# Part of a fused attention and feed-forward kernel in 512-token blocks, its second product further behind, and its first two slots interleaved

## The chip, the core and the metric

The kernel runs on one core of a Trainium2 chip. The time is device microseconds of the whole program, as the median of several runs. A profile shows one execution in detail; its span, from the first instruction to the last, is some 2 us shorter than the time, since starting and ending the program are not in it.

## What is computed

The reference is a sliding-window attention followed by a feed-forward layer with a smooth ReLU:

```python
B, H, S, D = 8, 8, 576, 64                 # q, k, v
scores = q @ k.T / sqrt(D), kept where |i - j| <= 32
attn = softmax(scores) @ v
x = attn.transpose(0, 2, 1, 3).reshape(4608, 512)
h = x @ w_in                               # 512 -> 2048
g = where(h >= 1, h, where(h <= -1, 0, (h + 1) ** 2 / 4))
out = g @ w_out                            # 2048 -> 512
```

The inputs and the output are float32; the kernel multiplies in bfloat16 and sums in float32.

## The kernel before

**The feed-forward part.** x is kept transposed, xT (128 partitions, 4 groups of the 512 features, and a ring of 2304 tokens, which is 4 batches). The work is divided into blocks of 256 tokens (t, 18 of them) and, in each, eight steps f of 256 of the 2048 hidden features. One block and one step are a *slot*, a = 8 t + f, 144 slots in all, written out in the loop at L482. In a slot:

- TensorE makes hp, 2 x 128 hidden features by 256 tokens, with 8 matmuls of 256 columns (L504). hp has two buffers in ps_h (one bank each); slot 6 takes one of ps_o's.
- ScalarE makes rr = relu(hp / 2 + 1/2) (L508), and VectorE makes mx = max(hp, rr) (L515) and gT = min(rr, 1) * mx (L516), which is the smooth ReLU. In the slots of two_on_act ScalarE squares rr (L512) and VectorE needs one operation (L513).
- TensorE multiplies earlier gT by w_out, 8 slots behind: in slot a a *quarter* a - 8, four of the 16 matmuls of 512 columns that one output tile of 128 tokens needs (L444). Early blocks go in half widths, pair (L460). When a tile is complete ScalarE copies it (L449), and SP's queue stores it. gT has three buffers of 256 tokens; op, the product's accumulator, has two.

The last eight rounds of the loop, slots 144 to 151, have the second product alone; the very last tile is made in two halves (L433), so that the first half's store is under way while the second is computed.

**Attention.** It is cut into steps that are hung onto slots in a table, at(slot, ...). A step is one `sums` (the product of weights and v, and the sum of weights, L293; then ln and exp(-x) on ScalarE, L299 and L300, for the reciprocal; then VectorE writes xT, L305, or L308 in a batch's last step) and one `scores` of the step after (L227; exp on ScalarE, L235; the mask on VectorE, L201). A batch has five: tokens 0 to 223 for two pairs of heads, 224 to 479 for two pairs, and 480 to 575 for all. The list sl gives the slots of the steps from number 6 on. TensorE's order within a slot is hp, sums, scores, quarter. VectorE's order is mx and gT of the slot, the mask, then, at the next flush(), xT, and only then the next slot's mx. ScalarE's order is rr, exp, ln, exp(-x), the output copy, the next rr. [...]

**Loads.** GpSimd issues all loads that turn float32 into bfloat16 (q, k, v, w_in, w_out), in one queue, at most eight in flight; those of the later batches are issued in the slots of the table `loads`, and SP transposes q and k by DMA (xps), 6 and 8 slots later. Both tables are tied to sl.

**The start.** Half of batch 0's first two head rows is loaded first, transposed on TensorE and used for slots 0 and 1 alone: casts of q, transposes of q and k, copies out of PSUM (L190), the scores with the mask added as a bias (add_mask, L206), sums, and xT for 256 tokens in two parts, y = 0 and y = 1. Matmuls on a tile of zeros (keep_warm, L336) fill TensorE's time between: 11, 3, 4, 2 and 7. v of batch 0 comes in four loads (L106), then w_in's columns by 256, the rest of batch 0's q and k, more of w_in (columns 512 to 767 for slot 2, 768 to 1023 for slot 3, 1024 to 1535 in two larger loads for slots 4 and 5, and so on), and w_out.

Of the kernel before, what the change touches and what calls it, by code (L numbers as in the profile page):

```python
# [7 lines left out]
FP = mybir.dt.float32  # L8
BF = mybir.dt.bfloat16
# [5 lines left out]
def kernel(  # L15
# [19 lines left out]
    nc = tc.nc  # L35
# [6 lines left out]
    TAIL = S - MAIN  # L42
    RING = 4 * S
    PAD = 32
    LONG = 2

    const = ctx.enter_context(tc.tile_pool(name="const", bufs=1))
# [2 lines left out]
    ptp = ctx.enter_context(tc.tile_pool(name="ptp", bufs=2))  # L50
    smp = ctx.enter_context(tc.tile_pool(name="smp", bufs=2))
    ewp = ctx.enter_context(tc.tile_pool(name="ewp", bufs=3))
    gtp = ctx.enter_context(tc.tile_pool(name="gtp", bufs=3))
    osp = ctx.enter_context(tc.tile_pool(name="osp", bufs=3))
    ps_h = ctx.enter_context(tc.tile_pool(name="ps_h", bufs=2, space=bass.MemoryType.PSUM))
    ps_s = ctx.enter_context(tc.tile_pool(name="ps_s", bufs=1, space=bass.MemoryType.PSUM))
# [11 lines left out]
    w_in = const.tile([128, 4, DFF], BF, name="w_in")  # L68
    w_out = const.tile([128, 16, DM], BF, name="w_out")
    xT = const.tile([128, NY, RING], BF, name="xT")  # L70
    qTs = [const.tile([128, PAD + NY * S], BF, name=f"qT{i}") for i in range(3)]

    ctx.enter_context(tc.manual_schedule())
# [24 lines left out]
            nc.gpsimd.dma_start(out=x[:, :, h], in_=src[b, NY * h:NY * h + NY].rearrange("y s d -> (y s) d")  # L98
                                .rearrange("(u p) d -> p u d", p=128))

    def load_v(b, n):
        if b not in vn:
            vn[b] = nat.tile([128, 2 * NC, 2, D], BF, name="vn", tag="vn", bufs=3)
        h, a = divmod(n, 2)
        y = NY * h + 2 * a
        nc.gpsimd.dma_start(out=vn[b][64 * a:64 * a + 64, :, h], in_=v[b, y:y + 2].rearrange("y s d -> (y s) d")  # L106
                            .rearrange("(c r) d -> r c d", r=64))

    def load_w_in(c0, c1, h):
        nc.gpsimd.dma_start(out=w_in[64 * h:64 * h + 64, :, c0:c1],  # L110
# [20 lines left out]
    P.affine_select(out=step, in_=step, compare_op=ALU.is_ge, fill=-1.0, base=-65, channel_multiplier=-1,  # L131
                    pattern=[[1, 257]])
    for n in range(4):
        load_v(0, n)
    V.memset(ones, 1.0)
    for t in qTs:
        V.memset(t[:, 0:PAD], 0.0)
# [4 lines left out]
    def put(todo):  # L142
        for fn, *x in todo:
            fn(*x)
# [1 line left out]
    w = [(load_w_in, c, c + 256, h) for c in range(0, 1024, 256) for h in range(2)]  # L146
    w += [(load_w_in, 1024, 1536, h) for h in range(2)]
    w += [(load_w_in, c, c + 256, h) for c in range(1536, DFF, 256) for h in range(2)]
    put(w[:4] + [(load_half, 1, t, h) for t in range(2) for h in range(2)] + w[4:12])
    put([(load_w_out, 0, 0, 4)] + w[12:])  # L150
    P.tensor_copy(band[HD[1], 0:128], band[HD[1], 64:192])
    for m, n, x in ((mask4, 8, 128), (mask8, 4, TAIL)):
# [55 lines left out]
                                 .to_broadcast([64, n, w]),  # L208
                                 start=True, stop=False, skip_group_check=True)

    def scores(b, ys, pars, cs, eng, pool=ps_s, w=128):

        if b not in pt:
            pt[b] = ptp.tile([128, 2, 2, 2, 512], BF, name="pt")
        ps = two_banks(pool)
        n = 0
        if eng is None:
            cols = (ys[1] - ys[0]) * (pars[1] - pars[0]) * (cs[1] - cs[0])
            add_mask([ps[:, h] for h in range(2)], cols, w)
        for y1 in range(*ys):  # L220
            for par in range(*pars):
                for c2 in range(*cs):
                    c = 2 * c2 + par
                    for a in range(2):
                        for h in range(2):
                            s0 = S * (y1 + 2 * a) + 64 * c
                            nc.tensor.matmul(ps[HD[a], h, w * n:w * n + w], kT[b][HD[h], s0:s0 + 64],  # L227
                                             qTs[b % 3][HD[h], PAD + s0 - 32:PAD + s0 - 32 + w],
                                             start=eng is not None, stop=True, skip_group_check=True)
                    n += 1  # L230
        p = pt[b][:, :, ys[0]:ys[1], pars[0]:pars[1], 128 * cs[0]:128 * cs[1] - 128 + w]
        m = 2 if n > cs[1] - cs[0] else 1
        p = p[:, :, ys[0] - ys[0]] if ys[1] - ys[0] == 1 else p[:, :, :, 0]
        like = "p h (y j) -> p h y j"
        A.activation(p, ps[:, :, :w * n].rearrange(like, y=m), AF.Exp, scale=D ** -0.5)  # L235
        mask(eng, p, mask4[:, :256 * n].rearrange("p (h j) -> p h j", h=2).rearrange(like, y=m))
# [79 lines left out]
    TB = 256  # L316
# [29 lines left out]
    with tc.tile_pool(name="ps_p", bufs=1, space=bass.MemoryType.PSUM) as ps_p:  # L346
        keep_warm(11, ps_h, "hp")

        V.memset(qkT(0, 0).rearrange("d (y s) -> d y s", y=NY)[:, :, S // 2:352], 0.0)
        for b in range(LONG):  # L350
            V.memset(qkT(b, 0).rearrange("d (y s) -> d y s", y=NY)[:, :, S - PAD:], 0.0)
        V.memset(qkT(0, 1).rearrange("d (y s) -> d y s", y=NY)[:, :, S // 2:320], 0.0)
        qn[0, 0] = cast(q32, "qb", 5)
        qq = [tpose(0, n, 0, (A.copy, V.tensor_copy)[n], tp1(ps_h)) for n in range(2)]
        for x in qq:
            x()
        kk = [tpose(0, n, 1, (A.copy, V.tensor_copy)[n], tp1((ps_n, ps_p)[n])) for n in range(2)]
        keep_warm(3, ps_h, "hp")
        for x in kk:
            x()  # L360
        scores(0, (0, 1), (0, 2), (0, 2), None)
        scores(0, (0, 2), (0, 1), (2, 3), None, ps_n, 32)
        scores(0, (1, 2), (0, 2), (0, 2), None, ps_p)
        keep_warm(4, ps_h, "hp")
        e0 = sums(0, 0, 0, TB)
        keep_warm(2, ps_h, "hp")
        e1 = sums(0, 1, 0, TB, ps_p)
        keep_warm(7, ps_h, "hp")
        e0()
        e1()  # L370
    ps_o = ctx.enter_context(tc.tile_pool(name="ps_o", bufs=2, space=bass.MemoryType.PSUM))
# [33 lines left out]
        at(a, seq[2 + n][0])  # L405
    for n, a in enumerate((18, 20, 26.5, 28)):
        at(a, seq[3 + n][1])
    sl = [30, 32, 35, 39, 42, 45, 49, 52, 56, 59, 62, 65, 69, 73, 77, 81, 84, 88, 92]
    sl += [96, 99, 103, 106, 110, 113, 116, 120, 124, 128]
    for n, a in enumerate(sl):  # L410
        at(a, seq[6 + n][0], seq[7 + n][1] if n < len(sl) - 1 else None)
    for t in range(2):
# [6 lines left out]
        for t in range(2):  # L419
            xps.setdefault(a + 6 + 2 * t, []).append((b, t))  # L420

    gT, op = {}, {}

    def quarter(x):

        tt, ff = divmod(x, 4)
        if tt == NT // 128 - 1:
            half, n = divmod(ff, 2)
            if n == 0:
                op[tt] = ps_o.tile([128, 256], FP, name="op", tag="op")  # L430
            cols = slice(256 * half, 256 * half + 256)
            for j in range(NF * n, NF * n + NF):
                nc.tensor.matmul(op[tt], gT[tt // 2][:, j, 128 * (tt % 2):128 * (tt % 2) + 128], w_out[:, j, cols],  # L433
                                 start=j == 0, stop=j == 2 * NF - 1)
            if n:
                osb = osp.tile([128, 256], FP, name="osb")
                A.copy(osb, op[tt])
                nc.sync.dma_start(out=out[128 * tt:128 * tt + 128, cols], in_=osb)
            return
        if tt not in op:  # L440
            op[tt] = ps_o.tile([128, DM], FP, name="op", tag="op"), []
        o, done = op[tt]
        for j in range(4 * ff, 4 * ff + 4):
            nc.tensor.matmul(o, gT[tt // 2][:, j, 128 * (tt % 2):128 * (tt % 2) + 128], w_out[:, j],  # L444
                             start=not done, stop=len(done) == 2 * NF - 1, skip_group_check=True)
            done.append(j)
        if len(done) == 2 * NF:
            osb = osp.tile([128, DM], FP, name="osb")
            A.copy(osb, o)  # L449
            nc.sync.dma_start(out=out[128 * tt:128 * tt + 128, :], in_=osb)  # L450

    def pair(x):
# [4 lines left out]
        o, done = op[half, p]  # L457
        for tt in range(2):
            for j in range(4 * g, 4 * g + 4):
                nc.tensor.matmul(o[:, tt], gT[p][:, j, 128 * tt:128 * tt + 128], w_out[:, j, 256 * half:256 * half + 256],  # L460
                                 start=not done, stop=len(done) == 4 * NF - 1, skip_group_check=True)
                done.append(j)
        if len(done) == 4 * NF:
# [15 lines left out]
        for end in todo:  # L479
            end()  # L480

    for a in range(NF * NB + NF):  # L482
        t, f = divmod(a, NF)
        eng = None if a < 14 else V
        post = [x for n, x in pairs if n == a] + [a - NF] * (a >= 2 * NF + 2)
        for b, x in loads.get(a, []):
            if x < 2:
                load_nat(b, x)
# [2 lines left out]
                    load_v(b, n)  # L491
        if a == 0 or a > 3:
            flush()
        if t < NB:
            if t not in gT:
                gT[t] = gtp.tile([128, 2 * NF, TB], BF, name="gT", tag="gT")
            r0 = TB * t % RING
            if a == 6:
                hp = ps_o.tile([128, 2, TB], FP, name="hp", tag="op")
            else:  # L500
                hp = ps_h.tile([128, 2, TB], FP, name="hp", tag="hp")
            for j in range(2):
                for n, kk in enumerate((0, 2, 1, 3)):
                    nc.tensor.matmul(hp[:, j], w_in[:, kk, 256 * f + 128 * j:256 * f + 128 * j + 128],  # L504
                                     xT[:, kk, r0:r0 + TB], start=n == 0, stop=n == 3)

            rr = ewp.tile([128, 2, TB], FP, name="rr")
            A.activation(rr, hp, AF.Relu, scale=0.5, bias=0.5)  # L508
            g = gT[t][:, 2 * f:2 * f + 2]
            mx = ewp.tile([128, 2, TB], FP, name="mx")  # L510
            if a in two_on_act:
                A.activation(mx, rr, AF.Square)  # L512
                V.scalar_tensor_tensor(g, hp, 1.0, mx, op0=ALU.max, op1=ALU.min)  # L513
            else:
                V.tensor_max(mx, hp, rr)  # L515
                V.scalar_tensor_tensor(g, rr, 1.0, mx, op0=ALU.min, op1=ALU.mult)  # L516
        flush()
        run(a)
        for x in post:
            (pair if x < 4 * 4 else quarter)(x)  # L520
        run(a + 0.5)
        for x in xps.get(a, []):
            xpose(*x)
# [30 lines left out]
```

The softmax here doesn't subtract the row's maximum and nothing guards it: scores larger than these inputs give would overflow.

## Time and profile before

| what | value |
|---|---|
| time, median of 3 runs | 308.69 us (308.67 to 309.4) |
| span of the profiled run | 306.7 us, granted TensorE clock 1.0 |
| busy: PE, DVE, ACT, POOL | 299.9, 242.1, 192.5, 77.4 us |
| hp, 256 columns (L504) | 1152 matmuls, 149.4 us busy |
| op, 512 columns (L444) | 496 matmuls, 126.9 us busy |
| gT's two operations on VectorE (L515, L516) | 137 each, 690 and 695 ns |
| rr on ScalarE (L508) | 144, 595 ns |
| idle time of TensorE that the waits view lists | 3.1 us |

A row's mean is the length of one instruction; matmuls are pipelined, so their lengths overlap, and the cost of one is better read from the distance of two starts. A group of the time line is named by its first start and the time to its last end, and what stands in brackets is the idle time of the engine before it and what ended that.

### The profile page before, as it was taken

What the parts mean: (1) busy time and instruction counts of PE and PEld (TensorE: products, weight loads), DVE (VectorE), ACT (ScalarE), POOL (GpSimd) and SP (SyncE); (2) the same over time, 40 slices, a digit from 0 to 9 for tenths busy, and PEclk for the clock granted to TensorE, in tenths of its full rate; (3) what the DMA queues carried; (4) which work ended last, traced back from release to release, by engine and by line L of the source; (5) the groups of instructions that cost most, each with busy time, mean ns of one, the idle gap of its engine ahead of it and who ended that gap; (6) DMA issues with size and microseconds to landing.
All of it is one profiled execution on the core that took longest, in us unless ns stands there. A gap on an engine that the chain in (4) does not pass through costs nothing.

```text
span 306.7 us, 8496 instructions
## 1 busy us (share of the span) xinstructions
PE 299.9 (98%) x3650; PEld 206.6 (67%) x3650; DVE 242.1 (79%) x376; ACT 192.5 (63%) x320; POOL 77.4 (25%) x92
## 2 busy tenths in 40 slices
PE   8989999999999999999999999999999999999995
PEld 3567878876666666666666666666666666666654
DVE  4278568888888888889888888889888888888760
ACT  3688886738856767666656666566676666554431
POOL 8799461028008106400450003700000000000000
PEclk9999999999999999999999999999999999999999
DMA  9999999999999999996899156990811010010111
GB/s 153 182 197 198 177 201 152 174 152 149 138 206 89 170 191 107 159 94 142 102 170 138 34 108 91 167 150 17 177 50 36 34 36 36 35 36 34 60 45 68
DMA packets 137173, 35.70 MB, mean 116 GB/s; under 512 B 122160, under 2 KB 132912, under 8 KB 137136
## 3 DMA queue, kind: packets, MB, share of 16 engines
q0 software_dynamic: 102976, 18.06, 83.2%
q1 hardware_dynamic: 34016, 16.81, 25.6%
q8 instruction: 28, 0.46, 0.6%
q10 hardware_dynamic: 144, 0.29, 0.3%
q14 instruction: 9, 0.07, 0.1%
HBM read 36.70 MB, written 9.44 MB: 150 GB/s over the span
## 4 chain that ended last, share of the span: by engine, by line
PE 89%; ACT 3%; DVE 2%; DMA 2%; issue 1%; POOL 1%; POOLq 0%; ACTq 0%
PE hp L504 39%; PE op L444 36%; PE bb L293 6%; PE op L460 4%; PE bb L227 2%; DMA vn<-in_v_dram 2%; PE op L433 1%; ACT pt L235 1%; POOL vn L106 1%; PE tp L187 1%; DVE xT L305 1%; ACT rc L300 1%; DVE mx L515 1%; ACT lr L299 1%; DVE gT L513 0%
## 5 line engine op out<-in xcount | busy, mean ns | idle before, releaser
L504 PE MATMUL hp<-xT,w_in 128*128 128x256 bf16 x1152 | 149.4, 273 | 1.7 <-DMA w_in<-in_moe_w_in_dram 0.8
L508 ACT ACTIVATE rr<-hp 128x512 f32<-128x512 f32 x144 | 85.7, 595 | 87.8 <-PE hp L504 87.7
L504 PEld LDWEIGHTS <-w_in 128*128 128x128 bf16 x1152 | 112.0, 98 | 41.1 <-issue 2.3
L444 PE MATMUL op<-w_out,gT 128*128 128x512 bf16 x496 | 126.9, 380 | 0.0
L515 DVE TENSOR_TENSOR mx<-hp,rr 128x512 f32<-128x512 f32 x137 | 94.5, 690 | 30.8 <-ACT rr L508 28.9
L516 DVE SCALAR_TENSOR_TENSOR gT<-rr,mx 128x512 bf16<-128x512 f32 x137 | 95.2, 695 | 4.7
L444 PEld LDWEIGHTS <-gT 128*128 128x128 bf16 x496 | 46.1, 98 | 34.8
L98 POOL DMA_DIRECT2D qn<-in_q_dram x12 | 14.6, 1221 | 111.4 <-DMA kT<-kn 107.5
L235 ACT ACTIVATE pt<-bb 128x1024 bf16<-128x1024 f32 (+1 forms) x33 | 32.7, 1002 | 5.0 <-PE bb L227 3.7
L305 DVE TENSOR_TENSOR xT<-bb,rc 128x512 bf16<-128x512 f32 (+1 forms) x32 | 21.0, 658 | 10.1 <-ACT rc L300 9.6
L106 POOL DMA_DIRECT2D vn<-in_v_dram x32 | 27.5, 891 | 4.9 <-DMA w_out<-in_moe_w_out_dram 4.2
L300 ACT ACTIVATE rc<-lr 128x512 f32<-128x512 f32 (+2 forms) x40 | 23.5, 587 | 1.3
L449 ACT COPY osb<-op 128x512 f32<-128x512 f32 x31 | 18.1, 583 | 8.7 <-PE op L444 8.3
L299 ACT ACTIVATE lr<-bb 128x512 f32<-128x512 f32 (+2 forms) x40 | 22.0, 551 | 0.4 <-PE bb L293 0.3
L201 DVE TENSOR_TENSOR pt<-pt,mask 128x1024 bf16<-128x1024 bf16 (+1 forms) x33 | 20.3, 614 | 0.5 <-ACT pt L235 0.5
L293 PE MATMUL bb<-pt,ones 64*64 64x256 bf16 (+3 forms) x352 | 19.6, 256 | 0.1
L293 PE MATMUL bb<-pt,vn 64*64 64x128 bf16 (+3 forms) x712 | 18.4, 204 | 0.1
L293 PEld LDWEIGHTS <-vn 64*64 64x64 bf16 x712 | 16.7, 107 | 0.3 <-DMA vn<-in_v_dram 0.3
L460 PE MATMUL op<-w_out,gT 128*128 128x256 bf16 x128 | 16.5, 273 | 0.0
L293 PEld LDWEIGHTS <-ones 64*64 64x64 bf16 x352 | 10.2, 105 | 8.9 <-issue 8.9
L98 POOL DMA_DIRECT2D kn<-in_k_dram x12 | 14.6, 1230 | 0.5 <-issue 0.5
L227 PE MATMUL bb<-qT,kT 64*64 64x128 bf16 (+1 forms) x520 | 13.1, 217 | 0.3 <-DVE kT L190 0.2
(59 smaller groups left out, 115.1 us busy)
## 6 DMA issues: line engine op xcount, KB each, us to landing
out_dram<-osb SPq DMA_DIRECT2D x35, 256.0 KB, 2.5
vn<-in_v_dram POOLq DMA_DIRECT2D x32, 144.0 KB, 10.2
qn<-in_q_dram POOLq DMA_DIRECT2D x12, 288.0 KB, 6.9
kn<-in_k_dram POOLq DMA_DIRECT2D x12, 288.0 KB, 8.9
w_in<-in_moe_w_in_dram POOLq DMA_DIRECT2D x12, 128.0 KB, 5.7
w_out<-in_moe_w_out_dram POOLq DMA_DIRECT2D x4, 256.0 KB, 6.6
w_out<-in_moe_w_out_dram POOLq DMA_DIRECT2D x2, 512.0 KB, 15.8
kh<-in_k_dram POOLq DMA_DIRECT2D x4, 144.0 KB, 5.1
```

Source lines behind the costliest of these rows:

```text
L98: nc.gpsimd.dma_start(out=x[:, :, h], in_=src[b, NY * h:NY * h + NY].rearrange("y s d -> (y s) d") .rearrange("(u p) d -> p u d", p=128))
L106: nc.gpsimd.dma_start(out=vn[b][64 * a:64 * a + 64, :, h], in_=v[b, y:y + 2].rearrange("y s d -> (y s) d") .rearrange("(c r) d -> r c d", ...
L235: A.activation(p, ps[:, :, :w * n].rearrange(like, y=m), AF.Exp, scale=D ** -0.5)
L293: nc.tensor.matmul(bb[HD[h], a, o + c0:o + c1], ones[HD[a]] if c is None else vn[b][HD[a], c, h], p(a, h), start=n == 0, stop=True, skip_g ...
L299: A.activation(lr[:, :, :D0], bb[:, :, D0:2 * D0], AF.Ln)
L300: A.activation(rc[:, :, :D0], lr[:, :, :D0], AF.Exp, scale=-1.0)
L444: nc.tensor.matmul(o, gT[tt // 2][:, j, 128 * (tt % 2):128 * (tt % 2) + 128], w_out[:, j], start=not done, stop=len(done) == 2 * NF - 1, s ...
L460: nc.tensor.matmul(o[:, tt], gT[p][:, j, 128 * tt:128 * tt + 128], w_out[:, j, 256 * half:256 * half + 256], start=not done, stop=len(done ...
L504: nc.tensor.matmul(hp[:, j], w_in[:, kk, 256 * f + 128 * j:256 * f + 128 * j + 128], xT[:, kk, r0:r0 + TB], start=n == 0, stop=n == 3)
L508: A.activation(rr, hp, AF.Relu, scale=0.5, bias=0.5)
L515: V.tensor_max(mx, hp, rr)
L516: V.scalar_tensor_tensor(g, rr, 1.0, mx, op0=ALU.min, op1=ALU.mult)
```

## The change

- WIDE = 72, 136: the slots from 72 to 135 work on two blocks of 256 tokens at a time. A slot is then 128 hidden features by 512 tokens: 4 matmuls of 512 columns. The number of slots, and the size of what ScalarE and VectorE do in each, stay.
- gT becomes one tile with room for four blocks of 256 tokens; home(t) says which of them block t has. In a wide slot VectorE writes two of them at once.
- The second product is divided into units, single matmuls. Up to slot 39 it goes as before. From slot 40 to 87 a slot has 4, 3 or 3 units in turn, then 4; so it is 8 slots behind at slot 40 and 16 from slot 88 on, and eight more rounds of the loop follow at the end.
- The steps of attention from number 14 on are 1 to 5 slots earlier (sl), and with them the loads and DMA transposes of batches 4 to 7.
- Slots 0 and 1 are made together: the parts with y = 0 of both, then the parts with y = 1 of both.
- The first bias (add_mask) is issued before k's copies are waited for; keep_warm is 11, 1, 3, 0 and 6.
- v of batch 0 is loaded in two parts, chunks 0 to 13 where it was, and chunks 14 to 17 after w_in's columns 512 to 767.

```diff
-    for n in range(4):
-        load_v(0, n)
+        load_v(0, n, 0, 14)
...
-    put(w[:4] + [(load_half, 1, t, h) for t in range(2) for h in range(2)] + w[4:12])
+    put(w[:4] + [(load_half, 1, t, h) for t in range(2) for h in range(2)]
+        + w[4:6] + [(load_v, 0, n, 14, 2 * NC) for n in range(4)] + w[6:12])
...
-        keep_warm(3, ps_h, "hp")
+        keep_warm(1, ps_h, "hp")
+        first = two_banks(ps_s)
+        add_mask([first[:, h] for h in range(2)], 4, 128)
         for x in kk:
             x()
-        scores(0, (0, 1), (0, 2), (0, 2), None)
+        scores(0, (0, 1), (0, 2), (0, 2), None, ready=first)
...
-        keep_warm(4, ps_h, "hp")
+        keep_warm(3, ps_h, "hp")
         e0 = sums(0, 0, 0, TB)
-        keep_warm(2, ps_h, "hp")
         e1 = sums(0, 1, 0, TB, ps_p)
-        keep_warm(7, ps_h, "hp")
+        keep_warm(6, ps_h, "hp")
...
-    sl = [30, 32, 35, 39, 42, 45, 49, 52, 56, 59, 62, 65, 69, 73, 77, 81, 84, 88, 92]
-    sl += [96, 99, 103, 106, 110, 113, 116, 120, 124, 128]
+    sl = [30, 32, 35, 39, 42, 45, 49, 52, 55, 58, 61, 64, 67, 70, 74, 77, 80, 84, 88]
+    sl += [91, 94, 97, 101, 105, 108, 111, 114, 118, 123]
...
+    def home(t):
+
+        return (3 - t % 4 if t % 4 in (0, 3) else t % 4) if WIDE[0] <= NF * t < WIDE[1] else t % 4
...
+        if j == 0:
+            op[tt] = ps_o.tile([128, DM], FP, name="op", tag="op")
+        nc.tensor.matmul(op[tt], gT[:, j, home(tt // 2), 128 * (tt % 2):128 * (tt % 2) + 128], w_out[:, j],
+                         start=j == 0, stop=j == 15)
...
+            if wide:
+                n, f = divmod(a - WIDE[0], 2 * NF)
+                t = WIDE[0] // NF + 2 * n
+                r0 = TB * t % RING
                 hp = ps_h.tile([128, 2, TB], FP, name="hp", tag="hp")
                 for n, kk in enumerate((0, 2, 1, 3)):
+                    nc.tensor.matmul(hp.rearrange("p n t -> p (n t)"), w_in[:, kk, 128 * f:128 * f + 128],
+                                     xT[:, kk, r0:r0 + 2 * TB], start=n == 0, stop=n == 3)
+                g = gT[:, f, home(t):home(t + 1) + 1:home(t + 1) - home(t)]
...
+                if a == 0:
+                    hps = [ps_h.tile([128, 2, TB], FP, name="hp", tag="hp") for _ in range(2)]
+                    for y in range(2):
+                        for f2 in range(2):
+                            project(hps[f2], f2, 0, [(j, y + 2 * m) for j in range(2) for m in range(2)], y == 0, y == 1)
...
+        if a >= 40:
+            n = (4, 3, 3)[a % 3] if a < 88 else 4
+            for x in range(done, done + n):
+                unit(x)
+            done += n
```

## The prediction

> **What bounds the kernel now.** I read four views in this order: the page (who is busy, and in which slices), TensorE's waits, the time line of the first 32 us, and the time lines of single slots later on.
>
> ```profile
> PE   8989999999999999999999999999999999999995
> PEclk9999999999999999999999999999999999999999
> DMA  9999999999999999996899156990811010010111
> ...
> L504 PE MATMUL hp<-xT,w_in 128*128 128x256 bf16 x1152 | 149.4, 273 | 1.7 <-DMA w_in<-in_moe_w_in_dram 0.8
> L444 PE MATMUL op<-w_out,gT 128*128 128x512 bf16 x496 | 126.9, 380 | 0.0
> ```
>
> TensorE has 9 in all slices but the first few and the last, at full clock; the DMA engines have 9 for the first 18 slices. So two things can set the end: TensorE's own work after the start, and, in the start, transfers. TensorE's waits over the whole span:
>
> ```profile
> PE z L336 <- DVE warm L126: 1.2, 1, 1.2
> PE hp L504 <- DMA w_in<-in_moe_w_in_dram: 0.8, 2, 0.6
> PE hp L504 <- DVE gT L513: 0.5, 1, 0.5
> PE hp L504 <- DVE xT L305: 0.4, 1, 0.4
> PE bb L227 <- DVE kT L190: 0.2, 1, 0.2
> ```
>
> Only 3.1 us, and TensorE's time line puts every one before 31 us. The last two that matter here are these:
>
> ```profile
> 22.39 1.03 PE L504 MATMUL hp<-xT,w_in 128*128 128x256 bf16 x8 [0.24 <-DMA w_in<-in_moe_w_in_dram]
> ...
> 30.30 1.03 PE L504 MATMUL hp<-xT,w_in 128*128 128x256 bf16 x8 [0.47 <-DVE gT L513]
> ```
>
> The first is slot 4, which waits for w_in's columns 1024 to 1535; the second is slot 9, which waits until VectorE has read slot 7's hp. From 30.30 to 303.3 us TensorE never waits to speak of; a stretch of the windows view shows who else is near:
>
> ```profile
> 60.00:80.00 20.00, 20.00 (x256) 14.21 (x254) 17.08 (x27) 13.19 (x22) 8.25 (x8) 1.00 1.70 156
> ```
>
> 20.00 of 20 us on PE, 17.08 on VectorE (third busy figure), 13.19 on ScalarE. Thus after 30.30 a microsecond of TensorE work is a microsecond of the end, unless an edit wakes a wait.
>
> [...] eight 256-column hp take 0.87 us to the next start, four 512-column op 0.86. [...] the longest gap here is 0.59 us and PEclk is 9 throughout, so leaving out six of the warm-up matmuls should not cost the clock.
>
> **The change part by part.**
>
> (1) 512-token blocks, slots 72 to 135. Each of 64 slots has 4 matmuls of 512 columns for 8 of 256: [...] 10 ns, times 64 = 0.64 us saved, all on the path. Weight loads halve, but PEld was busy 14.21 of 20 us and hidden. VectorE's and ScalarE's operations keep 128x512 elements; gT's new address pattern costs them nothing that I can see[...].
>
> (2) w_out up to 16 slots behind. From slot 40 to 87 a slot has 3.33 instead of 4 op matmuls; 32 matmuls move to after slot 151. TensorE's sum is the same. What was 1.737 us in a bare slot becomes 0.873 + 3.33 x 0.216 = 1.593 us, so VectorE must keep up. Three slots with one attention step cost TensorE 3 x 0.873 + 10 x 0.216 + 0.81 (the mean that an attention step adds to a slot, from five successive ones) = 5.59 us. VectorE, start to start when it has work: 1.33 us for mx and g (223.84 to 225.17), 0.60 for the mask, 0.54 for xT: 3 x 1.33 + 1.14 = 5.13. It fits, with 8% to spare. The end is as before: the last tile in two halves, copy, DMA. Nothing to add.
>
> (3) Attention earlier. The instant when an attention slot's scores are issued I call T (the next op's start). What follows is latency, not work:
>
> ```profile
> 94.70 1.04 PE L444 MATMUL op<-w_out,gT 128*128 128x512 bf16 x4
> ...
> 96.81 0.56 DVE L308 TENSOR_TENSOR xT<-bb,rc 128x384 bf16<-128x384 f32 x1
> ```
>
> This is slot 39, a batch's tail step (tokens 480 to 575). xT is done at 97.37 = T + 2.67: ScalarE's exp, ln and exp come first. In the new schedule the tail step of batch 4 is in slot 70, and slot 72 is the first wide block, tokens 2304 to 2815, that is up to token 511 of batch 4. It needs that xT. TensorE arrives there after 3 op, a hp block and 3 op: 6 x 0.216 + 0.873 = T + 2.17. The wait is 2.67 - 2.17 + 0.05 (the release, as from xT's end at 14.49 to hp at 14.54) = 0.55 us. The kernel before shows such a wait in small: slot 32 needs slot 30's xT,
>
> ```profile
> 78.81 0.62 DVE L305 TENSOR_TENSOR xT<-bb,rc 128x448 bf16<-128x448 f32 x1 [0.18 <-ACT rc L300]
> ...
> 79.20 1.10 PE L504 MATMUL hp<-xT,w_in 128*128 128x256 bf16 x8
> ```
>
> and its group lasts 1.10 instead of 1.04 us, though 8 op lie between instead of 6. Slot 120 has the same distance to slot 118, but there scores8's shorter exp, 8 op, and the rows that are needed third leave about 0.5 us; no wait. Where a step is 3 slots before, T + 3.9 meets xT at T + 3.0: none.
>
> The other buffer is hp: slot a+3 needs mx of slot a+1, which stands behind xT. In a full-width step without an output copy (slot 32, T = 81.03, mx to 84.65) mx ends at T + 3.62, against T + 10 x 0.216 + 2 x 0.873 = T + 3.91: none. With the output copy in the same slot it is later:
>
> ```profile
> 220.54 1.04 PE L444 MATMUL op<-w_out,gT 128*128 128x512 bf16 x4
> ...
> 222.74 0.57 ACT L449 COPY osb<-op 128x512 f32<-128x512 f32 x1
> ...
> 223.84 0.69 DVE L515 TENSOR_TENSOR mx<-hp,rr 128x512 f32<-128x512 f32 x1 [0.28 <-ACT rr L508]
> ```
>
> mx ends at 224.53 = T + 3.99. Counting 10 op in three slots, a copy falls in an attention slot between 40 and 88 only in slot 49: 3.99 + 0.05 - 3.91 = 0.13 us. Loads and DMA transposes move with the steps, 17 and some 10 slots ahead; slots shorten by 0.144, so 2.4 us less of lead; k's transpose for slot 56 (scores at 127.9) was issued at 112.4 and takes 5.1 to land, 10 us to spare: nothing. On SP the transposes go past output DMAs that have 4.8 slots between them instead of 4: nothing.
>
> (4) The start. Bias before k's copies, vn in 14 + 4 chunks, fewer warm-ups, and slots 0 and 1 interleaved by half of x shorten the chain vn, sums, ln, exp, xT, hp, k's transposes by an estimated 0.8 to 1.0 us: 0.16 at the scores (8.37 to kT's end 8.15 + 0.05), 0.36 of waiting for the last vn inside the first sums (0.92 us long, the second 0.56), 0.43 at hp, the rest as q and k of the other half land earlier. But slot 4 waits for w_in, and the bytes that are queued ahead of it are the same: v's second part is put before columns 768 to 1535. The DMA engines are full from 4 to beyond 50 us, so it lands no earlier, and slot 4 starts at 22.39 again. From there TensorE runs without a gap to slot 7's hp (27.04 to 28.08), ScalarE's two operations on it (28.12, 28.75 to 29.38) and VectorE's (0.69) end at 30.09, where the trace has 30.25. So at slot 9 at most 0.15 us of it is left. POOL issues four more DMAs, 4 x 0.63 us less 4 x 0.06 (each first part is shorter) less 1.12 of idle time: 1.2 us later in its queue for w_in and w_out. Behind them stand w_out's next part and the loads of batch 1. w_in's issue leads its landing by 5.7 us (median), so this is hidden by the backlog; bound: 0 to 1.2 us, I take 0.
>
> Sum against the profiled span: 306.7 - 0.64 + 0.55 + 0.13 - 0.15 = 306.6. The runs' median is 308.69, 2.0 above the span (its own run 308.5); so 308.6.
>
> **The rivals.** (a) The start's saving reaches the end: 1.0 instead of 0.15, so 307.7, and 307.2 if slot 72 doesn't wait either. For: the chain that ended last runs through vn and not through w_in. Against: w_in's wait at 22.39. It decides if those columns land 0.8 us earlier. (b) Slower: POOL's late issues delay w_in and slot 4. Beyond 0.15 us of float every delay counts; 1.2 us gives 309.8. For: POOL waits 1.12 us for an earlier w_in at 14.56 already. Against: full DMA engines. (c) Slower: VectorE becomes the bound in slots 40 to 88. It decides when three slots cost it over 5.59 us; not overlapped at all they are 3 x 1.42 + 0.69 + 0.69 = 5.64, and with 0.2 us of waiting for ScalarE in each, 15 steps lose 0.25 each: 3.7 us, 312. (d) Wide blocks save nothing per column: 309.2.
>
> **How the numbers follow.** The likeliest, the sum above with its small errors, 0.63 (its own range 308.0 to 309.2); (a) 0.19, (b) 0.10, (c) 0.05, (d) 0.03. A measurement tells 0.3%, 0.93 us, from no change. Faster takes (a) and little else, 0.20; slower (b), (c), 0.15; the same 0.65. For 8 in 10 the range must take in most of (a) and (b): 307.4 to 309.9.
>
> **What would show it.** Right: hp at slot 4 starts at about 22.4 with a wait for w_in, though slots 0 and 1 end 1 us earlier; slot 9 near 30.1; one wait of TensorE for xT of about 0.55 us at slot 72; PE full elsewhere; 863 ns a wide block. Wrong: slot 4 at 21.5 (a) or 23.5 (b); many waits of hp for mx between 100 and 190 us (c).

## The result and the profile after

The changed kernel takes 313.02 us (median of 6 runs, 311.72 to 314.02) against 308.68 us of the kernel before (6 runs, 308.5 to 309.4): a ratio of 1.0133, 95% interval 1.0108 to 1.0159. It is 4.3 us slower. The profiled execution took 313.08 us with a span of 311.3 us, against 308.5 and 306.7 before, so the two traces hold the difference: 4.6 us.

The page of the changed kernel, granted TensorE clock and DMA share in 40 slices of 7.8 us:

```profile
PE   8857999999999999999999999999999999999995
PEclk9997999999999999999999999999999999999999
DMA  9999999999999999999995799861001010000121
```

TensorE has a 5 and a 7 in slices 3 and 4 (15.6 to 31.1 us), and the clock digit of slice 4 is 7. From slice 5 on the row is 9s, as before. The loss lies in the first 31 us. TensorE's waits over the whole span:

```profile
PE hp L489 <- DMA w_in<-in_moe_w_in_dram: 4.3, 2, 3.1
...
PE hp L513 <- DVE xT L310: 0.4, 1, 0.4
```

The wait for w_in was 0.8 us in two pieces before; it is 4.3 us now, one piece of 3.1. (A row "op <- issue" of 4.7 us in 30 pieces in the same view is no loss: in those slots records of single matmuls are missing (L449 has 460 of them for its 496 weight loads), and the intervals from slot to slot are the same as in runs where all are there.) The time line of TensorE, at slots 3, 4, 5 and 9:

```profile
20.43 1.03 PE L489 MATMUL hp<-xT,w_in 128*128 128x256 bf16 x8 [1.19 <-DMA w_in<-in_moe_w_in_dram]
...
25.57 1.23 PE L489 MATMUL hp<-xT,w_in 128*128 128x256 bf16 x8 [3.13 <-DMA w_in<-in_moe_w_in_dram]
...
27.64 1.89 PE L489 MATMUL hp<-xT,w_in 128*128 128x256 bf16 x8
...
34.83 1.03 PE L489 MATMUL hp<-xT,w_in 128*128 128x256 bf16 x8 [0.33 <-DVE gT L536]
```

Slot 4 starts at 25.57 instead of 22.39: 3.18 us. Slot 5's eight matmuls take 1.89 us, near twice the usual 1.05. Slot 9 starts at 34.83 instead of 30.30: 4.53 us, nearly the whole loss. From slot 9 to the end it is 276.5 us after and 276.4 before. The trace records when the granted clock changes; it does so at 26.27 and 29.68 us. The windows view shows the 3.41 us ahead of that stretch and the stretch itself (the first busy figure is PE's, the number behind POOL's is PEclk):

```profile
22.86:26.27 3.41, 0.70 (x7) 0.67 (x8) 1.65 (x3) 1.25 (x3) 2.52 (x5) 1.00 1.33 177
26.27:29.68 3.41, 3.41 (x47) 2.10 (x49) 2.01 (x3) 1.83 (x4) 2.90 (x5) 0.50 1.45 195
```

TensorE is busy all of 26.27 to 29.68 us, at half of its clock. From slot 4 to slot 9 it needs 9.26 us (34.83 - 25.57) instead of 7.91 (30.30 - 22.39): 1.35 us. So a start of slot 4 that is 3.18 us late and 1.35 us of slow clock make the 4.53.

Where the wait comes from stands in the chain of the stretch from 12 to 28 us, read upwards from the late hp:

```profile
8.46 5.46 DMA qh<-in_q_dram
...
14.21 1.22 POOL vn L107 x2
...
15.60 0.61 POOL w_in L111
...
16.46 1.20 POOL w_in L111 x2
17.66 7.77 DMA w_in<-in_moe_w_in_dram
...
25.57 1.23 PE hp L489 x8
```

The last load of w_in's columns 1024 to 1535 is issued at 17.66 and lands at 25.43 (before: 15.77 and 22.26). Ahead of it POOL stands until 14.21 before it may issue the third of v's four small loads: it waits for a load of q that was issued eight places earlier and landed at 13.93. In the traces of both kernels every load of GpSimd's queue from the ninth on (76 before, 80 after) is issued after the eighth before it has landed, and none sooner than 0.28 us after (here 13.93 to 14.21). The records of those up to 21 us name eight semaphores in turn, 99 to 106, and each load waits for its own before it is issued; so this is a wait that the program holds. The issue of the last load is 1.9 us late but its landing 3.2. The DMA part of the window from 17 to 23 us, kernel before, then the changed one:

```profile
DMA packets 1871, 1.19 MB, mean 198 GB/s; under 512 B 98, under 2 KB 1870, under 8 KB 1870
```

```profile
DMA packets 1228, 0.78 MB, mean 129 GB/s; under 512 B 232, under 2 KB 1227, under 8 KB 1227
```

0.41 MB less is moved in these 6 us, 2.1 us' worth at the old rate. The DMA row of the page has 9 for this stretch in both kernels and does not tell the two apart. The GB/s do.

### The profile page after: what moved, and what is told of

Read it like the earlier page. It is cut to its first block, busy times and chain, and to the rows that moved or that the text cites. A ratio compares the mean times of both kernels' runs of the same rounds, so it can differ in the third digit from the quotient of the medians.

```text
span 311.3 us, 7939 instructions
## 1 busy us (share of the span) xinstructions
PE 294.3 (95%) x3350; PEld 181.8 (58%) x3388; DVE 240.6 (77%) x376; ACT 191.9 (62%) x320; POOL 79.1 (25%) x96
## 4 chain that ended last, share of the span: by engine, by line
PE 87%; DMA 4%; POOL 3%; issue 2%; ACT 1%; DVE 1%; POOLq 0%; ACTq 0%
PE op L449 33%; PE hp L489 21%; PE hp L513 18%; PE bb L295 6%; PE op L464 4%; DMA w_in<-in_moe_w_in_dram 2%; PE bb L229 2%; DMA qh<-in_q_dram 2%; POOL vn L107 1%; POOL w_in L111 1%; PE op L440 1%; PE tp L189 1%; ACT pt L237 1%; ACT rr L532 0%; POOL kh L86 0%
## 5 line engine op out<-in xcount | busy, mean ns | idle before, releaser
L449 PE MATMUL op<-w_out,gT 128*128 128x512 bf16 x460 | 119.6, 379 | 5.0 <-issue 4.7
L489 PE MATMUL hp<-xT,w_in 128*128 128x256 bf16 x640 | 84.1, 275 | 5.5 <-DMA w_in<-in_moe_w_in_dram 4.3
L489 PEld LDWEIGHTS <-w_in 128*128 128x128 bf16 x640 | 62.2, 98 | 26.0 <-issue 5.1
L449 PEld LDWEIGHTS <-gT 128*128 128x128 bf16 x496 | 46.0, 98 | 45.3
L513 PE MATMUL hp<-xT,w_in 128*128 128x512 bf16 x256 | 65.7, 379 | 0.4 <-DVE xT L310 0.4
L513 PEld LDWEIGHTS <-w_in 128*128 128x128 bf16 x256 | 25.0, 98 | 30.8 <-issue 0.7
L107 POOL DMA_DIRECT2D vn<-in_v_dram x36 | 29.7, 856 | 5.7 <-DMA w_out<-in_moe_w_out_dram 3.9
```

The costliest lines, as they stand in the source:

```text
L107: nc.gpsimd.dma_start(out=vn[b][64 * a:64 * a + 64, c0:c1, h], in_=v[b, y:y + 2].rearrange("y s d -> (y s) d") .rearrange("(c r) d -> r c ...
L449: nc.tensor.matmul(op[tt], gT[:, j, home(tt // 2), 128 * (tt % 2):128 * (tt % 2) + 128], w_out[:, j], start=j == 0, stop=j == 15)
L513: nc.tensor.matmul(hp.rearrange("p n t -> p (n t)"), w_in[:, kk, 128 * f:128 * f + 128], xT[:, kk, r0:r0 + 2 * TB], start=n == 0, stop=n == 3)
```

## The experiments

Theory Q: v's second part (four loads of 32 KB, half of the eight places) leaves GpSimd's queue too little to move, so the DMA engines run short and w_in's columns 1024 to 1535 come late. Rival F: the other edits of the start (fewer warm-ups, slots 0 and 1 interleaved). Rival S: the part from slot 40 on. Later, rivals inside Q: the number of DMAs and POOL's time for them; the 256-byte pieces of v.

All numbers in one table; "slot 4" and "slot 9" are the starts of their hp, "landed" is the last landing of columns 1024 to 1535, GB/s the mean from 17 to 23 us. Each ratio is to runs of the kernel before beside that kernel's own (medians 308.61 to 308.73 us).

| kernel | us | ratio to before, 95% | slot 4 | slot 9 | landed | GB/s |
|---|---|---|---|---|---|---|
| before | 308.68 | | 22.39 | 30.30 | 22.26 | 198 |
| changed | 313.02 | 1.0133 (1.0108-1.0159) | 25.57 | 34.83 | 25.43 | 129 |
| 1 v whole | 308.45 | 0.9998 (0.9989-1.0006) | 22.30 | 30.18 | 22.16 | 198 |
| 2 only v's split | 311.95 | 1.0108 (1.0072-1.0145) | 24.75 | 34.01 | 24.61 | 137 |
| 3 warm in the gap | 312.06 | 1.0106 (1.0085-1.0126) | 26.08 | 33.85 | 25.13 | 123 |
| 4 four spare loads | 312.62 | 1.0130 (1.0079-1.0182) | 26.96 | 36.27 | 26.82 | 98 |
| 5 second part later | 310.36 | 1.0064 (1.0037-1.0091) | 21.49 | 31.13 | 21.33 | 185 |
| 6 tail step in 69 | 308.07 | 0.9974 (0.9963-0.9985) | 22.36 | 30.27 | 22.22 | 199 |
| 7 from slot 40 alone | 308.90 | 1.0007 (0.9996-1.0018) | 23.18 | 31.00 | 23.05 | 191 |
| 8 both 5 and 6 | 309.60 | 1.0027 (1.0013-1.0042) | 22.22 | 31.68 | 22.08 | 165 |
| 9 two spare loads | 310.59 | 1.0063 (1.0040-1.0086) | 23.84 | 31.98 | 23.70 | 145 |
| 10 w_in merged | 312.84 | 1.0135 (1.0090-1.0179) | 25.92 | 33.68 | 25.79 | 104 |
| 11 6 and w_in merged | 308.43 | 0.9983 (0.9974-0.9991) | 22.82 | 30.82 | 22.68 | 195 |
| 12 8 and w_in merged | 308.99 | 1.0013 (0.9997-1.0030) | 21.67 | 30.72 | 21.29 | 186 |
| 13 v on ScalarE's queue | 310.51 | 1.0057 (1.0044-1.0071) | 24.58 | 32.85 | 22.73 | 191 |
| 14 four large spare | 313.07 | 1.0140 (1.0121-1.0160) | 26.59 | 34.46 | 25.52 | 174 |

The times are medians of all runs; slots, landings and GB/s are of the one profiled execution. Where the start is disturbed the runs mostly spread over 2 to 5 us (changed kernel: 2.3), so differences of under 1 us between such kernels are not read. Part of the spread is the clock: of experiment 4's runs, those with a mean granted clock of 0.995 took 313.95 and 314.46 us, those with 0.998 and 1.0 took 311.29 and 311.26.

### Which part of the change costs it

**1: v whole again.**

```diff
-        load_v(0, n, 0, 14)
+        load_v(0, n)
-        + w[4:6] + [(load_v, 0, n, 14, 2 * NC) for n in range(4)] + w[6:12])
+        + w[4:12])
```

> The changed kernel with v of batch 0 loaded in one part again; everything else of the change stays. Theory Q (v's second part, four DMAs of 32 KB in GpSimd's queue ahead of w_in's columns 768 to 1535, delays w_in): slot 4's hp starts near 22.4 us as in the kernel before, slot 9's near 30.1, total 308.0 to 308.8 us. Rival F (the other edits of the start, fewer warm-ups above all, cost the time through the TensorE clock): slot 9 stays near 34.8, total about 313. Rival S (512-token blocks and w_out 16 slots behind cost it): slot 9 near 30.1 but total still 311 to 313.

308.45 us: the loss is gone with this one edit. Slot 4's line is that of the kernel before again:

```profile
22.30 1.03 PE L489 MATMUL hp<-xT,w_in 128*128 128x256 bf16 x8 [0.25 <-DMA w_in<-in_moe_w_in_dram]
```

**2: the kernel before with only v's split**, the same edit made there.

```diff
-        load_v(0, n)
+        load_v(0, n, 0, 14)
-    put(w[:4] + [... load_half ...] + w[4:12])
+    put(w[:4] + [... load_half ...] + w[4:6] + [(load_v, 0, n, 14, 2 * NC) for n in range(4)] + w[6:12])
```

> The kernel before with v of batch 0 loaded in two parts as in the changed one, and nothing else of the change. Theory Q: slot 4's hp waits for w_in and starts at 24.5 to 26 us, the clock falls after the wait, slot 9 near 33 to 35, total 311.5 to 313.5 us. Rivals F and S: slot 4 at 22.4 to 22.6, total 308.5 to 309.

311.95 us, as Q expected: 3.3 of the 4.3 us without anything else of the change. F and S fall. In two of the four runs the mean clock was 0.995 (312.22 and 313.57 us), in two 1.0 (310.77 and 311.69); in all six of the changed kernel it was 0.993 to 0.995. That goes with the smaller loss. The lines show the wait and the slow clock again:

```profile
24.75 1.11 PE L505 MATMUL hp<-xT,w_in 128*128 128x256 bf16 x8 [2.24 <-DMA w_in<-in_moe_w_in_dram]
26.71 1.89 PE L505 MATMUL hp<-xT,w_in 128*128 128x256 bf16 x8
```

**7: the part from slot 40 on alone**, with v whole and the start as before.

```diff
 (changed kernel, with these taken back)
-        first = two_banks(ps_s)
-        add_mask([first[:, h] for h in range(2)], 4, 128)
-                    for y in range(2):
-                        for f2 in range(2):
-                            project(hps[f2], f2, 0, ...)
+        keep_warm(...)  (the five calls of before)
```

> The kernel before with the 512-token blocks, the attention slots and w_out 16 slots behind of the changed kernel, and with the whole start of before (warm-ups, order of slots 0 and 1, v in one part). By the prediction's steps 1 to 3: -0.64 + 0.55 + 0.13, so 308.6 to 308.8 us, within 0.15 of the kernel with v whole. If VectorE limits slots 40 to 88: 309.5 to 312. If wide blocks save more than 10 ns each and the waits are smaller: 308.0.

308.90 us, no measurable difference from before (0.1 over the range written down, and 0.45 over the kernel with v whole, where within 0.15 was expected). From slot 9 to the end it takes 276.5 us (307.5 - 31.00), as in the changed kernel and within 0.1 of the kernel before.

### How much of it is the clock

**3: warm-up matmuls in the gap**, on the changed kernel.

```diff
                     hps = [pool.tile([128, 2, TB], FP, name="hp", tag=tag)]
+                    for _ in range(12 if a == 4 else 0):
+                        nc.tensor.matmul(hps[0].rearrange("p n t -> p (n t)"), warm[:, :128], warm, start=True, stop=True)
```

> The changed kernel with twelve warm-up matmuls of 512 columns (2.6 us at full clock) between slot 3 and slot 4's hp, written into the hp bank that slot 4's first matmul overwrites. w_in lands no earlier. If the 3.13 us of idle lowered the clock, slots 4 to 8 run at full speed again: slot 9's hp near 33.5 instead of 34.83, total 311.5 to 312 us. If the slow matmuls from 27.6 to 29.5 us have another cause than the idle time, slot 9 stays at 34.8 and the total at 313.

312.06 us, just over the range; by the times alone the 1 us is not clear of the spread, so the trace decides. The warm-ups fill the gap and slot 4's hp has its 1.04 us:

```profile
23.48 2.76 PE L528 MATMUL hp<-warm 128*128 128x512 bf16 x11
26.08 1.04 PE L489 MATMUL hp<-xT,w_in 128*128 128x256 bf16 x8
```

Slot 4 to slot 9 takes 7.77 us at full clock, against 9.26 in the changed kernel. So the clock's share, 1.35 us by the comparison of the traces, is shown by taking it away; the wait stays. Not all of it was gained, since the warm-ups outlast the wait: w_in has landed at 25.13, slot 4 starts at 26.08.

### What in the split: the number, the bytes or the places

**4: four spare loads in the kernel before**, of one chunk of v each, into a tile that nobody reads.

```diff
+    spare = const.tile([128, 1, 2, D], BF, name="spare")
-        ... + w[4:12])
+        ... + w[4:6] + [(load_spare, n) for n in range(4)] + w[6:12])
```

> The kernel before with four extra loads of 16 KB (chunk 17 of v, into a spare tile that nobody reads) in GpSimd's queue at the place of v's second part; v itself is whole. It adds 64 KB, 0.34 us at the 190 KB/us of this stage. Count (four more DMAs take turns in the queue and POOL's issue time, whatever they carry): slot 4's hp at 24.5 to 26 us, total 311 to 313. Bytes (only what is moved ahead of w_in matters): slot 4 at 22.7, total 309 us.

The sizes there are those read in float32; the profile counts what is written, in bf16: 8 KB each, 32 KB in all, 0.17 us. They cost 4.0 us, as much as v's second part (in the fastest of the four runs still 2.6 us). The bytes are nothing; that there are four is enough. The window from 17 to 23 us:

```profile
DMA  9876010105699999999979356779996998587799
...
DMA packets 1109, 0.59 MB, mean 98 GB/s; under 512 B 293, under 2 KB 1108, under 8 KB 1108
```

Here the engines stand nearly still from 17.6 to 18.4 us: the next load of w_in is issued at 17.04, 0.28 us after the landing of the eighth before it (16.76), and its bytes move from 18.4 on.

**9: two of them.**

> The kernel before with two spare loads of 16 KB instead of four at the same place: the dose. If the loss grows in proportion to the DMAs: about half of the 4.0 us of the four, 310.6 us, slot 4's hp near 24.7. If the backlog covers some of them first (POOL's lead over the landings was 5 us, and 1.1 us of its time there is waiting): little is lost, slot 4 at 22.4 to 23, total 308.6 to 309.3.

310.59 us: half of the loss of four, and the GB/s lie between (145). Slot 4 is at 23.84 in the profiled execution, not 24.7. No reserve covers the first ones.

**10: two loads fewer ahead**, the changed kernel with w_in's columns 0 to 511 in two loads instead of four.

```diff
-    w = [(load_w_in, c, c + 256, h) for c in range(0, 1024, 256) for h in range(2)]
+    w = [(load_w_in, 0, 512, h) for h in range(2)]
+    w += [(load_w_in, c, c + 256, h) for c in range(512, 1024, 256) for h in range(2)]
```

> The changed kernel, v in two parts as there, but w_in's columns 0 to 511 in two DMAs of 512 columns instead of four of 256: the same bytes in the same order, two DMAs fewer ahead of columns 768 to 1535. Theory count: POOL reaches those columns at least 1.2 us earlier, slot 4's hp at 22.5 to 24 instead of 25.57, no cold clock, total 308.5 to 310.5 us. Theory bytes (256-byte pieces of v are what is slow, not their number of DMAs): slot 4 stays at 25.5, total 313.

312.84 us, no gain, so fewer DMAs ahead alone do not help. POOL's time line says why:

```profile
12.44 0.61 POOL L107 DMA_DIRECT2D vn<-in_v_dram  x1 [1.42 <-DMA w_in<-in_moe_w_in_dram]
13.73 1.33 POOL L107 DMA_DIRECT2D vn<-in_v_dram  x2 [0.67 <-DMA w_in<-in_moe_w_in_dram]
15.54 0.61 POOL L107 DMA_DIRECT2D vn<-in_v_dram  x1 [0.49 <-DMA qh<-in_q_dram]
```

The 1.2 us that POOL has gained are spent in waits of 1.42, 0.67 and 0.49 us (changed kernel: 0.63 before v's loads). POOL is held by landings, and not by its own time: in the changed kernel it issues the two loads of columns 1024 to 1535 0.39 and 0.32 us after the landing of the eighth before, where 0.28 is the least in the traces of both kernels. The expectation offered the 256-byte pieces of v as the other reading; that is tested by the next two.

**14: four large spare loads** at the place of the small ones (sixteen chunks each; 128 KB as written, not the 256 KB of the expectation, which are the bytes read).

```diff
-    spare = const.tile([128, 1, 2, D], BF, name="spare")
+    spare = const.tile([128, 16, 2, D], BF, name="spare")
```

> The kernel before with four spare loads at the same place as the 16 KB ones, of 256 KB each. Four DMAs more in the queue again, but each with as much to move as a w_in load, so 1 MB or 5.4 us more bytes ahead of columns 768 to 1535. If the number of DMAs (POOL's time for them) is what costs: 5.4 us and the 4 us of the small ones on top, slot 4 at 31 us. If what costs is that small loads leave little queued: the engines stay at 190 to 200 KB/us, slot 4 at 27.5 to 28.2, and the packets keep their durations.

With 0.5 MB ahead, columns 1024 to 1535 land at 25.52, 3.3 us late, about what half a megabyte takes at the 154 GB/s that were moved from 17 to 20 us. The small ones, with a sixteenth of the bytes, made them land at 26.82, 4.6 us late; that execution was the slowest of its four (314.46 us), so the 1.3 us between the two are not read, only that so few bytes cost as much. The last of these columns is issued at nearly the same time in both (19.02 and 18.93), with the small ones 0.28 us after the eighth before landed, with the large ones 0.85. So with the large ones POOL's time does count, and still the 3.3 us are no more than the bytes take. The engines run through:

```profile
DMA packets 4834, 1.04 MB, mean 174 GB/s; under 512 B 4047, under 2 KB 4833, under 8 KB 4833
```

The rate is 174 GB/s although 4047 packets are under 512 B, so short pieces by themselves don't bring it down to 98. The total, 313.07 us, was not what was measured for: here slot 3 waits 2.84 us for columns 768 to 1023 behind half a megabyte that nobody needs, and the clock falls as well.

**13: v's second part on ScalarE's queue**, as float32, turned to bf16 by VectorE in slot 3; batch 4's tail step in slot 69.

```diff
+        if a == 0:
+            for n in range(4):
+                ...
+                nc.scalar.dma_start(out=v32[...], in_=v[0, y:y + 2]...[:, 14:])
+        if a == 3:
+            V.tensor_copy(vn[0][:, 14:], v32)
```

> The changed kernel with batch 4's tail step in slot 69 and with v's second part on ScalarE's DMA queue: four float32 loads issued after slot 0's operations, turned to bf16 by one VectorE copy in slot 3. The same small pieces, but none of GpSimd's places is taken and POOL issues no DMA for them. If the loss is that small loads fill the eight places of GpSimd's queue: no loss, slot 4's hp at 21.8 to 22.8, total 307.8 to 308.8 us. If dividing v is what costs (256-byte pieces, whatever queue): slot 4 at 24 to 25.5, total 311 to 312.5.

Half of the expectation came (columns 1024 to 1535 in time, the total not): 191 GB/s from 17 to 23 us, and columns 1024 to 1535 landed at 22.73 instead of 25.43, with the same small pieces on their way. So it is the places in GpSimd's queue. The total missed (310.51 us), for two new reasons. The first is in ScalarE's time line:

```profile
14.85 2.63 ACTq L546 DMA_DIRECT2D v<-in_v_dram  x4
17.53 0.60 ACT L533 ACTIVATE rr<-hp 128x512 f32<-128x512 f32 x1 [2.08 <-PE tp L190]
```

Issuing four loads took ScalarE 2.63 us, in which slot 1's relu waited, though its hp was long done. VectorE's operation on it and the copy of q that stands behind it are late, and TensorE waits 1.45 us for that copy, until 20.23. The second reason is the clock; it falls at 20.26, as the windows on both sides show:

```profile
16.85:20.26 3.41, 1.35 (x23) 0.96 (x17) 1.48 (x4) 2.70 (x5) 3.31 (x6) 1.00 1.25 193
20.26:23.68 3.42, 3.42 (x44) 2.02 (x47) 1.82 (x3) 1.75 (x4) 3.02 (x5) 0.50 1.35 188
```

From 20.23 to slot 4 (24.58) TensorE needs 4.35 us for what takes it 2.76 in experiment 6 (19.38 to 22.36, less a wait of 0.22). So slot 4 is late by ScalarE's issues and by 1.6 us of slow clock, not by w_in.

### Can the changed kernel be kept

**5: v's second part behind columns 768 to 1535.**

```diff
-        + w[4:6] + [(load_v, 0, n, 14, 2 * NC) for n in range(4)] + w[6:12])
+        + w[4:10] + [(load_v, 0, n, 14, 2 * NC) for n in range(4)] + w[10:12])
```

> The changed kernel with v's second part four places later in GpSimd's queue: behind w_in's columns 768 to 1535 instead of ahead of them. Theory Q (what costs is four small DMAs ahead of columns that are awaited): columns 1024 to 1535 are issued at about 15.2 and land at 21.5 to 22.3 us, slot 4's hp starts at 21.6 to 22.4, its sums may wait up to 0.6 us for v; slot 9 at 29.6 to 30.6, total 307.8 to 308.9 us. Rival (four small DMAs anywhere ahead of 20 us let the engines run short, so the delay only moves to columns 1536 to 1791 and slot 6): slot 6's hp 1 to 3 us late, total 309.5 to 311.5.

The rival was right, a slot later than it said. Slot 4 starts at 21.49, 0.9 us earlier than before, and doesn't wait, and slot 6 is not late either; but then slot 7's hp and the w_out matmuls after it wait:

```profile
PE op L464 <- DMA w_out<-in_moe_w_out_dram: 1.2, 1, 1.2
PE hp L489 <- DMA w_in<-in_moe_w_in_dram: 0.5, 1, 0.5
```

w_out's first and w_in's last columns are now late (from 23 to 29 us 143 GB/s are moved, 196 in the kernel before), and 310.36 us is 1.6 slower than before (308.73 beside it).

**6: v whole, and batch 4's tail step in slot 69**, one slot earlier.

```diff
-    sl = [30, 32, 35, 39, 42, 45, 49, 52, 55, 58, 61, 64, 67, 70, 74, ...
+    sl = [30, 32, 35, 39, 42, 45, 49, 52, 55, 58, 61, 64, 67, 69, 74, ...
```

> As the changed kernel with v whole, and with batch 4's tail step in slot 69 instead of 70, three slots ahead of the first 512-token block. The wait of 0.4 us (predicted 0.55) at slot 72 should go: 308.0 us against 308.45 of the kernel that only has v whole. If another wait takes its place (two steps in slots 67 and 69 crowd VectorE): no gain, 308.4.

308.07 us, ratio 0.9974: faster than both kernels, and the lowest median of all. TensorE's wait for xT at the first 512-token block is gone from its waits, and from slot 9 to the end it takes 275.9 us (306.2 - 30.27), 0.5 less than the others.

**8: both 5 and 6.**

> Both: v's second part behind columns 768 to 1535 and batch 4's tail step in slot 69. If the gains add: 0.4 us below the kernel with only v's second part moved, so 307.4 to 308.4 us, the fastest of all. If the moved part still delays slot 6: as that kernel less 0.4.

309.60 us, near the second of the two readings (310.4 less 0.4): the moved part still costs, so the gains don't add to a best version.

**11 and 12: w_in's first 512 columns in two loads**, on 6; and on 8, there with the last 512 in two as well.

> The kernel with v whole and the tail step in slot 69 (308.07 us), with columns 0 to 511 of w_in in two DMAs. If the engines are limited by bytes there, slot 4 stays at 22.3 and the total at 308.0 to 308.2. If POOL's turns still cost something with v whole (it waits 1.1 us before columns 768 to 1023): slot 4 at 21.9 to 22.2, slot 9 0 to 0.3 us earlier, total 307.7 to 308.0. If slots 0 and 1 wait for the larger DMA: 308.3 to 309.

> v's second part behind columns 768 to 1535, the tail step in slot 69, and w_in's columns 0 to 511 and 1536 to 2047 in two DMAs each instead of four: as many DMAs as with v whole. Theory count: slot 4 at 21.3 to 21.8 without a wait, none at slots 6 to 8 either, slot 9 at 29.3 to 29.9, total 307.3 to 307.9 us, the fastest. If the position or the bytes of v's second part cost it: slots 6 to 8 wait for w_in or w_out, 308.5 to 309.6.

11 gives 308.43 us, no gain over 6 (the two intervals overlap, so it is not shown to be slower either): slots 0 and 1 wait 1.77 us for the larger load, the third of the cases written down. 12 missed: 308.99 us instead of at most 307.9. In the profiled execution (308.41 us) slot 4 starts at 21.67 without a wait, but slot 6 waits 0.38 us for w_in and the w_out matmuls after it 0.27, and the runs spread from 307.95 to 311.99. With as many DMAs as when v is whole, v's second part still disturbs (0.6 us over 11): again not the number.

## Why the prediction was wrong

It was wrong in one step, the last of part (4), and it had no term for the slow clock that follows from that step.

- *Step (4), "hidden by the backlog; bound: 0 to 1.2 us, I take 0".* This failed, in the value and in the bound. The backlog was taken as a time, the 5.7 us between issue and landing, which does not say how many bytes are under way. In these runs the rate went with what the loads in flight still had to move: from 17 to 23 us it was 98 GB/s with four of 8 KB put ahead (experiment 4), 129 with v's four of 32 KB (the changed kernel), 174 with four of 128 KB (experiment 14) and 198 with none (before). When the first load of columns 1024 to 1535 was issued in the kernel before (15.16), six loads of 128 to 144 KB ahead of it had not landed; in the changed one (17.06), two of w_in's, the tail of a third, and v's four of 32 KB. In the kernel before, experiment 4 fills four places with next to nothing, and experiment 14 with full loads. The term was 1.9 us of late issue, 1.3 us more between issue and landing, and 1.35 us of slow clock. The trace had shown POOL waiting 1.12 us "<- DMA w_in" at 14.56; it was counted as idle time that four issues could fill, while it was the queue's limit, and four more loads tie each later issue to a landing four loads later.
- *Rival (b), "POOL's late issues delay w_in and slot 4", 309.8 us.* The late issue and the place were right, the size was not (1.2 instead of 4.5 us). It was priced as POOL's own time, where 1.9 us came from waiting for landings, and it had nothing for engines that run short and for the clock. Its chance of 0.10 was too low, and the range ended at 309.9.
- *"Leaving out six of the warm-up matmuls should not cost the clock."* Right as it stands: slots 0 to 3 run at full speed after (1.00 in the windows from 12 to 26.27 us). But the sum had no term for the clock behind a longer wait, and the trace of before, whose longest gap in the slots is 0.59 us at a full clock, does not show what such a wait does. Measured in the changed kernel, the clock rises at 5.79 us, falls at 26.27, six times 3.41 us later, and rises again 3.41 us after that; in experiment 13 it was low for 3.42 us (20.26 to 23.68). TensorE was not idle all through the 3.41 us before the fall: 0.70 us of matmuls in them did not keep the clock up in the changed kernel, and 1.35 did not in experiment 13, where the waits were of 0.62 and 1.45 us.
- *Start: "slot 4 starts at 22.39 again", "the front chain shortens".* The front did end about 1.1 us earlier (the first two hp blocks at 15.09 instead of 16.23). With v whole slot 4 starts at 22.30 and slot 9 at 30.18: 0.12 us gained where 0.15 was said. That this fits so well is in part luck, since with the start as before slot 9 was at 30.30 in one execution and at 31.00 in another (experiment 7). That the bytes hold slot 4 was right, as long as the engines are full.
- *Steps (1) to (3), -0.64 + 0.55 + 0.13.* The sum is 0.04; measured from slot 9 to the end it is under 0.1 (276.5 against 276.4). The 10 ns of step (1) are in the traces: from the start of eight hp to the next op it is 873 ns in the kernel before (the median), from the start of a wide block's four 863 in the changed one. The wait at slot 72 is there, with the mechanism given:

```profile
158.50 0.81 PE L449 MATMUL op<-w_out,gT 128*128 128x512 bf16 x3
159.70 1.02 PE L513 MATMUL hp<-xT,w_in 128*128 128x512 bf16 x4 [0.38 <-DVE xT L310]
```

The view gives 0.38 us of idle time, but the records of matmuls overlap; from start to start it is 1.20 us, where three op without a wait take 0.65 (experiment 6, 153.94 to 154.59). So hp stands 0.55 us until xT ends, as said, and the wide block lasts 0.86 us, as computed (the next op starts at 160.56). Experiment 6 takes the wait away, and from slot 9 to the end it is 0.5 us faster than before, where -0.64 + 0.13 was left of the sum. The 0.13 us at slot 49 does not show in the waits. Rival (c), VectorE the bound, has no support: no wait of hp for mx between slots 40 and 88.

Without v's split the prediction's number would have stood: 308.45 us measured, 308.6 said.

One thing is open. After the engines have run short, packets stay slow for some 5 us more, though POOL issues ahead again: w_in's 1 KB packets take 98 ns in the kernel before at 19 to 20 us, and 135 ns on average, 858 at most, in the changed one at 20 to 21 us; there the mean of each microsecond from 19 to 25 is 102 to 138 ns. No run tells why. The 1.3 us between issue and landing probably belong to it.

## What to carry to other kernels

When a queue holds a fixed number of transfers (eight here), count the bytes in flight ahead of the load that is awaited, not the bytes in the whole queue: one load divided in two takes two places, and small loads ahead of a large one that is waited for can empty the engines (98 GB/s with four of 8 KB, 198 without). Read the GB/s by stretch, for the busy share of the page can stay at 9 while the engines starve, as it did at 129 GB/s. Where TensorE waits for a transfer, add what its clock loses behind the wait (1.35 us here), and count all its idle time in a stretch rather than the longest wait (experiment 13 lost its clock with 0.62 and 1.45 us in one of 3.41); and before moving a load to a computing engine's queue, look for what that engine must do meanwhile (four loads took ScalarE 2.63 us).

## What was not expected of the hardware

- Four loads of 8 KB cost 4.0 us of the kernel's time, as much as four of 128 KB at the same place (4.4 us): from 17 to 23 us 98 GB/s were moved with the small ones, 174 with the large ones.
- The granted clock fell to 0.50 in five of the 16 profiled executions behind waits of the start, each time for one stretch of 3.41 us. Dividing each trace into stretches of that length from its first change of clock, TensorE was busy 0.27 us (4), 0.70 (changed kernel), 0.76 (14), 1.17 (2) and 1.35 (13) in the stretch before; with 1.60 us (3) or more it never fell. So it was not the longest single wait that decided: experiment 10 kept its clock with waits of 2.19 and 2.03 us, each of which lay across the border of two stretches, and 13 lost it with 1.45 and 0.62 us in one. These are five cases; where between 1.35 and 1.60 us the border lies, and whether it is one of busy time at all, is not shown.
- A load of 64 x 4 pieces of 256 bytes kept ScalarE's instruction stream for 0.66 us (2.63 us for four), as long as POOL needs for one of its own (0.61). Four loads on ScalarE's queue kept the DMA engines at 191 GB/s, and the kernel still lost 1.8 us, because ScalarE was on the path and the clock fell to 0.50 behind the wait.
